# In an attention, routing and bilinear kernel, the split remainders and x transposes a unit later, w3 transposes in every second unit

## The chip, the cores and the metric

The kernel runs on one core of a Trainium2 chip. The metric is device microseconds (us) of one execution, here the median over several executions. The engines are named as in the profile: PE (TensorE matmul), DVE (VectorE), ACT (ScalarE), POOL (GpSimd) and SP (SyncE, which here only issues transfers).

## The reference

Four steps follow each other: windowed causal attention, a routed expert network (each of 2304 tokens goes to one of 8 experts), and a bilinear layer. Cut to what matters:

```python
# q, k, v: (4, 8, 576, 64) f32; window 128, a slope per head
attn = softmax(where(mask, q @ k.T * scale + bias, -1e9)) @ v     # -> x (2304, 512)
e_idx = argmax(x @ w_gate + modality_bias[modality_id], axis=1)   # 8 experts
x = gate[:, None] * (relu(x @ w1[e_idx]) @ w2[e_idx])             # 512 -> 1024 -> 512
h = ((x @ m_w1) * (x @ m_w2)) @ m_w3                              # float64 weights, 1024 x 1024
out = (h @ m_wout).astype(float32)                                # 512 columns
```

The kernel multiplies the last two weights with each other first (W = m_w3 @ m_wout), and it does so in the gaps of the attention. This product is called pw below, its pieces w3 and wo.

## The kernel before

**Units.** The attention runs in 40 units, numbered 0 to 39. Unit `i` is `units[i] = (b, c, hq)`: batch `b`, chunk `c` of 128 query rows (the fifth chunk of a batch, `c = NF`, has 64), and four of the eight heads. Two units make a chunk, an even one and then an odd one. The loop has 42 rounds, and round `i` writes the work of several units, in this order: `scores` and `softmax` of unit `i` (tile S in PSUM; DVE adds the bias and takes the row minimum into p, L458; ACT takes the exponential, L463); in odd rounds `attend` of the two units before (tile av); `p_transposes` of unit `i-1` (PT, copied by ACT to pT); then jobs from tables, and the transposes of later work. On PE the order is that of the program: each matmul is tied behind the one before (`after_pe`). On DVE, ACT and POOL a scheduler sets the order, from its own plan of the times, within the data's needs. In the block stage behind the loop the scheduler orders PE too.

**Splits.** All products of fp32 tiles are made of a rounded high part and a remainder (names end in h and l). In the first nine chunks (`pe_lo`) the remainder of q and k is made on PE: `split_k` copies the high part on ACT (kTh, qTh, L351) and puts `split_rest` on the list `rests`; `split_rests()` later issues one matmul with a negative identity into the same PSUM tile (ktp<-kTh,id_k and qtp<-qTh,id_q), and ACT copies the rest out (kTl, qTl, L319). In later chunks DVE subtracts instead (kTl L304, qTl L306).

**Transposes of x.** Behind `attend` ACT copies av to xT (L517; the 64-row tail to xTt, L525). `chunk_done` puts `gate_logits` on the list `todo`: four transposes (xtp), the gate product (lg), then on DVE x, lr, ls and the logit. Behind the last tile of a group (`GROUPS`) it puts `route` there too: some 15 small DVE operations that end in hot_b and hcum, two small matmuls that count tokens (rk<-hot_b and rk<-hcum), and scatters on POOL. One entry of `todo` is taken a round.

**w3 pieces.** A piece `j` of 16 is loaded (`load_w3`, SP, 512 KB, three buffers raw_w shared with the wo pieces), converted from float64 (`cvt_w3`, four DVE operations L753, L757, L760, L763 and one POOL addition L766), transposed on PE (`w3_transposes`, tile w3tp) and split by ACT and DVE (w3h, w3l). `w_step` then is three matmuls into pw (56 steps in all; `W_STEPS` says how many a round has, 35 of them in the loop, and 21 behind it cover the latency of routing). `LEAD` says how many rounds ahead of its first step a piece is loaded, converted and transposed, and `READY` gives these rounds for the last pieces by hand.

**Buffers in PSUM.** The tag A has two buffers, which ktp, qtp, qktp, lg, w3tp and rk take in turn; S has two and a unit uses both; av and xtp share the one buffer of V; pw has G.

**Behind the loop** stand the expert blocks (ph, py), and then the bilinear layer (p, po).

Of the kernel before, what the change touches and what calls it, by code (L numbers as in the profile page):

```python
# [27 lines left out]
WO_AT = [4, 5, 7, 8, 10, 11, 13, 15]  # L28
TP_AFTER = 20
M_PRE = 3  # L30
LEAD = [4, 3, 1]
LATE = 5
HB = 8
EARLY, M_PER, W_PER = 3, 3, 2

EDGE_L, EDGE_R = 96, 992
JS, BT = (3, 1)
W_STEPS = [0, 0, 0, 0, 0, 0, 0, 0, 0, 0, 0, 0, 0, 1, 1, 1, 1, 1, 2, 1, 1, 1, 2, 1, 1, 1, 2, 1, 1, 1, 2, 1, 1, 1, 2, 1, 1, 1, 2, 1, 1, 1]

IDLE_TO, IDLE_N = 12, 2  # L40

PW_FIRST = 3
GROUPS = [[0, 4], [4, 5], [9, 4], [13, 3], [16, 1], [17, 1]]

READY = [(28, 31, 34), (29, 32, 36), (30, 33, None), (31, 34, None), (32, 35, None), (33, None, None)]


def f32(ap):
# [4 lines left out]
def kernel(  # L53
# [728 lines left out]
    def split_wout(g):  # L782
        x = to_f32(w_p, st_w.pop(("o", g)), f"wo_{g}", x=wo_last if g == NG else None)
        if g < NG:
            nc.scalar.copy(woh[:, g, :], x)
            nc.gpsimd.tensor_tensor(
                out=wol[:, g, :], in0=x, in1=f32(woh[:, g, :]), op=ALU.subtract
            )

    def load_w3(i):  # L790
        fc, u = divmod(i, 2)
        st_w["3", i] = load_f64(
            w_p, m_w3[fc * P : (fc + 1) * P, u * HALF : (u + 1) * HALF], f"w3_{i}"
        )

    def cvt_w3(i):
        st_w["x", i] = to_f32(w_p, st_w.pop(("3", i)), f"w3_{i}")

    def w3_transposes(i, sp=split):
        x = st_w.pop(("x", i))  # L800
        h = w_p.tile([P, 4, P], F32R, tag="w3h", name=f"w3h_{i}", bufs=3)
        l = w_p.tile([P, 4, P], F32R, tag="w3l", name=f"w3l_{i}", bufs=3)
        tp = pst("A", [P, 4, P], f"w3tp_{i}")
        for j in range(4):
            pe(
                tp[:, j, :], lhsT=x[:, j * P : (j + 1) * P], rhs=ident, is_transpose=True,
                start=(j == 0 or sp is split), stop=(j == 3 or sp is split),
            )
        n = 3 if i % 2 else 4
        if i % 2:  # L810
            last["a"] = nc.scalar.copy(w3_last[:, i // 2, :], tp[:, 3, :])
        sp(h[:, :n, :], l[:, :n, :], tp[:, :n, :])
        st_w["T", i] = (h, l)

    def w_piece(k):

        fc, g = divmod(k, NG)
        return 2 * fc + g // 4, g % 4 == 0
# [96 lines left out]
    def chunk_done(b, c):  # L915
        if c == NF and b % 2 == 0:
            return
        i = tidx[b, c]
        g, j = tile_group[i]
        todo.append(lambda: gate_logits(i, g, j))  # L920
        if j == groups[g][1] - 1:
            todo.append(lambda: route(g, *groups[g]))
# [5 lines left out]
    def at(i, f, jobs=w_jobs):  # L928
        jobs.setdefault(max(i, 0), []).append(f)

    for g in range(NMC):
        if g >= WO_PRE:
            at(WO_AT[g] - 2, lambda g=g: load_wout(g))
        at(WO_AT[g], lambda g=g: split_wout(g))
    ks = 0
    for i, m in enumerate(W_STEPS):
        for _ in range(m):
            j, first = w_piece(ks)
            if first:
                if j >= W3_PRE:  # L940
                    at(i - LEAD[0], lambda j=j: load_w3(j))
                at(i - LEAD[1], lambda j=j: cvt_w3(j))
                at(i - LEAD[2], lambda j=j: w3_transposes(j), w_tps)
            at(i, lambda n=ks: w_step(n), w_steps)
            ks += 1
    n_w, k_in = NMC * NG, ks
    j_in, n_j = w_piece(k_in - 1)[0] + 1, 2 * NMC
    assert w_piece(k_in) == (j_in, True) and j_in + len(READY) == n_j
    for r, (u_load, u_cvt, u_tp) in enumerate(READY):
        at(u_load, lambda j=j_in + r: load_w3(j))  # L950
        if u_cvt is not None:
            at(u_cvt, lambda j=j_in + r: cvt_w3(j))
        if u_tp is not None:
            at(u_tp, lambda j=j_in + r: w3_transposes(j), w_tps)
    def idle(i):
        if i <= IDLE_TO:
            idle_work(IDLE_N)
# [6 lines left out]
            jobs.pop(i, None)  # L964

    for i in range(nu + 2):
        if 1 <= i < nu:
            scores(*units[i])
            softmax(*units[i])
        if i % NQ == 1 and i >= 3:  # L970

            for u in (units[i - 3], units[i - 2]):
                attend(*u)
            chunk_done(*units[i - 2][:2])
        if 1 <= i < nu + 1:
            p_transposes(*units[i - 1])
        with tc.issue_after(last["sm"].ins):
            run(w_jobs, i)
        run(w_steps, i, 1)

        ci = i // NQ + 1 if i > 1 else i
        if i and (i == 1 or i % NQ == 0) and ci < len(chunks):
            transposes(*chunks[ci])
            idle(i)
            run(w_steps, i, 1)
        if i % NQ == 1 and i // NQ + 2 < len(chunks):
            load_chunk(*chunks[i // NQ + 2])
        for f in extras.pop(i, []):
            f()
        if i % NQ:  # L990
            idle(i)
        if todo:
            todo.pop(0)()
        split_rests()
        run(w_tps, i)
        run(w_steps, i)
    strict[0] = False
    pe_mark = last["pe"]
# [403 lines left out]
```

## Time and profile before

| | |
|---|---|
| median of 3 executions | 792.93 us (790.63 to 793.63) |
| the profiled execution | 785.28 us, of it the span of the trace 783.5 us |
| PE busy | 742.3 us, 95% of the span |
| attention and routing | 0 to about 250 us; expert blocks 250 to 474; bilinear layer to the end |

A window of the trace gives each engine's busy time in a stretch, a row of waits says which engine waited for what, and a row of the timeline gives start, length and, in brackets, the idle time of the engine just before it with what ended it. Starts are counted from the start of the span.

### The profile page before, as it was taken

Reading aid. Unit: us, or ns where it says so; the run is one execution under the profiler, and the core shown is the slowest. Engines: PE = TensorE matmul, PEld = TensorE weight load, DVE = VectorE, ACT = ScalarE, POOL = GpSimd, SP = SyncE. Lnnn points to the kernel's source line nnn. Section 1 sums busy time; section 2 is a strip of 40 time slices with the busy share of each in tenths; the row PEclk is TensorE's granted clock in tenths of the full one; section 3 lists DMA queues with packets and bytes.
Section 4 is the critical chain, followed back from the end, with each engine's and each line's share of the span. In section 5 each row is a group of like instructions: output and inputs, shape, how many; then the busy total and the mean of one; then the engine's idle time right before and its main releaser. Section 6 shows DMA issues by size and latency. Waiting matters only on the chain. (4 is left out here: it accounts for less than half of the span.)

```text
span 783.5 us, 11943 instructions
## 1 busy us (share of the span) xinstructions
PE 742.3 (95%) x4424; PEld 618.2 (79%) x4424; DVE 388.8 (50%) x1015; ACT 325.7 (42%) x757; POOL 111.3 (14%) x140
## 2 busy tenths in 40 slices
PE   7898898996999999999999999999999999999996
PEld 4775786884877888888888885888888888888895
DVE  4687877787874575666666416550221122022030
ACT  6776767675645334333434224541222122122121
POOL 3235211213232220200100000001000000100101
PEclk9998999998999999999999999999999999999998
DMA  7866555455316765573844014002002001100000
GB/s 160 219 180 162 155 152 139 112 145 99 119 29 186 238 210 189 173 244 116 259 157 164 27 41 122 0 9 87 13 1 81 27 1 37 44 1 1 40 15 27
DMA packets 100503, 81.93 MB, mean 105 GB/s; under 512 B 69850, under 2 KB 83418, under 8 KB 100437
## 3 DMA queue, kind: packets, MB, share of 16 engines
q1 hardware_dynamic: 93925, 66.52, 30.0%
q0 software_dynamic: 3632, 9.66, 3.7%
q10 hardware_dynamic: 2880, 4.92, 1.7%
q8 instruction: 36, 0.59, 0.3%
q14 instruction: 30, 0.25, 0.1%
HBM read 66.36 MB, written 14.54 MB: 103 GB/s over the span
## 5 line engine op out<-in xcount | busy, mean ns | idle before, releaser
L1294 DVE TENSOR_TENSOR a<-a,p 128x512 f32<-128x512 f32 (+1 forms) x40 | 25.4, 634 | 188.8 <-PE p L293 188.8
L304 DVE TENSOR_TENSOR fwl<-fw,fwh 128x1024 fp32r<-128x1024 f32 x40 | 48.8, 1225 | 75.9 <-ACT fwh L302 66.0
L463 ACT ACTIVATE p<-p,mn 128x256 f32<-128x256 f32 (+2 forms) x144 | 67.9, 474 | 29.0 <-DVE mn L458 26.7
L302 ACT ACTIVATE fwh<-fw 128x1024 fp32r<-128x1024 f32 x40 | 42.2, 1061 | 89.1 <-PE ph L293 66.9
L293 PE MATMUL ph<-xbh,fwh 128*128 128x480 f32 x160 | 61.3, 384 | 0.0
L293 PE MATMUL ph<-xbh,fwl 128*128 128x480 f32 x160 | 61.0, 381 | 0.0
L293 PE MATMUL ph<-xbl,fwh 128*128 128x480 f32 x160 | 60.8, 380 | 0.0
L293 PE MATMUL py<-hl,fwh 128*128 128x480 f32 x160 | 60.4, 381 | 0.0
L302 ACT ACTIVATE abh<-a 128x512 fp32r<-128x512 f32 (+1 forms) x40 | 23.5, 588 | 87.2 <-DVE a L1294 87.2
L293 PE MATMUL p<-x2h,m0h 128*128 128x512 f32 (+1 forms) x160 | 59.0, 369 | 0.0
L293 PE MATMUL p<-x2l,m0h 128*128 128x512 f32 (+1 forms) x160 | 58.8, 368 | 0.0
L293 PE MATMUL p<-x2l,m1h 128*128 128x512 f32 (+1 forms) x160 | 58.8, 368 | 0.0
L293 PE MATMUL p<-x2h,m1l 128*128 128x512 f32 (+1 forms) x160 | 58.8, 368 | 0.0
L293 PE MATMUL p<-x2h,m0l 128*128 128x512 f32 (+1 forms) x160 | 58.8, 368 | 0.0
L293 PE MATMUL p<-x2h,m1h 128*128 128x512 f32 (+1 forms) x160 | 58.7, 368 | 0.0
L293 PE MATMUL py<-hh,fwl 128*128 128x480 f32 x160 | 57.9, 380 | 0.0
L293 PE MATMUL py<-hh,fwh 128*128 128x480 f32 x160 | 57.6, 379 | 0.0
L293 PE MATMUL po<-Wl,abh 128*128 128x512 f32 (+1 forms) x152 | 57.3, 378 | 0.0
L293 PE MATMUL po<-Wh,abh 128*128 128x512 f32 (+1 forms) x152 | 57.3, 378 | 0.0
L293 PE MATMUL po<-Wh,abl 128*128 128x512 f32 (+1 forms) x152 | 56.8, 378 | 0.0
L1316 POOL DMA_INDIRECT out_dram<-o,idg x17 | 16.4, 964 | 279.2 <-ACT o L1311 274.7
L458 DVE CUSTOM_DVE_ANT_0 p<-S,bias 128x256 f32<-128x256 f32 (+1 forms) x128 | 42.7, 384 | 13.8 <-PE S L293 13.2
(230 smaller groups left out, 1630.8 us busy)
## 6 DMA issues: line engine op xcount, KB each, us to landing
fw<-in_moe_w_dram SPq DMA_DIRECT2D x40, 512.0 KB, 4.9
raw_w<-in_moe_w_dram SPq DMA_DIRECT2D x16, 512.0 KB, 4.0
raw_m<-in_moe_w_dram SPq DMA_DIRECT2D x16, 512.0 KB, 3.7
ys_dram<-y ACTq DMA_DIRECT2D x20, 240.0 KB, 4.3
vr<-in_v_dram SPq DMA_DIRECT2D x16, 256.0 KB, 3.3
raw_wo<-in_moe_w_out_dram SPq DMA_DIRECT2D x8, 512.0 KB, 3.8
xs_dram<-x SPq DMA_DIRECT2D x16, 256.0 KB, 3.4
yt<-ys_dram SPq DMA_DIRECT2D x8, 512.0 KB, 4.5
```

Source lines behind the costliest of these rows:

```text
L293: last["pe"] = nc.tensor.matmul(*args, **kw)
L302: last["a"] = nc.scalar.activation(out=hi, in_=src, func=AF.Copy, scale=scale)
L304: last["v"] = nc.vector.tensor_tensor(out=lo, in0=src, in1=f32(hi), op=ALU.subtract)
L458: last["sm"] = nc.vector.tensor_tensor_reduce(out=p[:, j, t, :nk], in0=s[j][:, t, :nk], in1=bi, scale=1.0, scalar=BIG, op0=ALU.add, op1=AL ...
L463: nc.scalar.activation(out=p[:, j, t, :nk], in_=p[:, j, t, :nk], func=AF.Exp, scale=-1.0, bias=m1, accum_out=sm[:, col : col + 1],)
L1294: nc.vector.tensor_tensor(out=a[:, :nt], in0=a[:, :nt], in1=pp[1][:, :nt], op=ALU.mult)
L1316: sc = nc.gpsimd.indirect_dma_start(out=dst, out_offset=bass.IndirectOffsetOnAxis(ap=idx, axis=0), in_=o[:, ds_], in_offset=None,)
```

## The change

The work is the same but for two fillers (`idle`) that are left out in round 1. The round is written in another order: `split_rests()` is called in the odd rounds behind `p_transposes`, so one round later than the transposes it belongs to (in round 1 it stays in its round); `chunk_done` moves from the head of the odd round to its end, so `gate_logits` comes in the next even round and `route` in the odd round behind that; `w3_transposes` come in odd rounds alone, ahead of the next chunk's transposes. The tables `LEAD`, `W_STEPS` and `READY` are others: loads are issued two rounds ahead of the conversion and in the order of the pieces, steps begin with two in odd rounds and one in even ones, and of the last rounds some have none.

```diff
-LEAD = [4, 3, 1]
+LEAD = [5, 3, 1]
-W_STEPS = [0, 0, 0, 0, 0, 0, 0, 0, 0, 0, 0, 0, 0, 1, 1, 1, 1, 1, 2, 1, 1, 1, 2, 1, 1, 1, 2, 1, 1, 1, 2, 1, 1, 1, 2, 1, 1, 1, 2, 1, 1, 1]
+W_STEPS = [0, 0, 0, 0, 0, 0, 0, 0, 0, 0, 0, 0, 0, 2, 1, 2, 1, 2, 1, 2, 1, 2, 1, 2, 1, 2, 1, 2, 1, 2, 1, 2, 1, 1, 0, 1, 0, 0, 0, 1, 1, 1]
-READY = [(28, 31, 34), (29, 32, 36), (30, 33, None), (31, 34, None), (32, 35, None), (33, None, None)]
+READY = [(26, 29, 31), (28, 30, 33), (29, 31, 35), (30, 32, None), (31, 33, None), (32, 34, None), (33, None, None)]
...
-                at(i - LEAD[2], lambda j=j: w3_transposes(j), w_tps)
+                at((i - LEAD[2] - 1) | 1, lambda j=j: w3_transposes(j), w_tps)
...
     for i in range(nu + 2):
+        odd = i % NQ == 1
         if 1 <= i < nu:
             scores(*units[i])
             softmax(*units[i])
-        if i % NQ == 1 and i >= 3:
+        if odd and i >= 3:
             for u in (units[i - 3], units[i - 2]):
                 attend(*u)
-            chunk_done(*units[i - 2][:2])
         if 1 <= i < nu + 1:
             p_transposes(*units[i - 1])
         with tc.issue_after(last["sm"].ins):
             run(w_jobs, i)
+        if odd:
+            split_rests()
         run(w_steps, i, 1)
-
+        if todo:
+            todo.pop(0)()
+        run(w_tps, i)
         ci = i // NQ + 1 if i > 1 else i
-        if i and (i == 1 or i % NQ == 0) and ci < len(chunks):
+        if i and (i == 1 or not odd) and ci < len(chunks):
             transposes(*chunks[ci])
             idle(i)
-            run(w_steps, i, 1)
-        if i % NQ == 1 and i // NQ + 2 < len(chunks):
+            if i == 1:
+                split_rests()
+        elif odd:
+            idle(i)
+        if odd and i >= 3:
+            chunk_done(*units[i - 2][:2])
+            if i > nu:
+                run(w_steps, i)
+                while len(todo) > 1:
+                    todo.pop(0)()
+        if odd and i // NQ + 2 < len(chunks):
             load_chunk(*chunks[i // NQ + 2])
         for f in extras.pop(i, []):
             f()
-        if i % NQ:
-            idle(i)
-        if todo:
-            todo.pop(0)()
-        split_rests()
-        run(w_tps, i)
         run(w_steps, i)
```

In the order lists below a name has its tile and a running number; PT_1_0 is chunk 1 and the first half of its heads.

**First place: PE, units 2 and 3 (batch 0).** Before, behind the transposes of chunk 2 (ktp, qtp) in unit 2:

```order
L298 MATMUL PT_0_1_1_326<-ident,p_0_1_247 128x128 x2
L293 MATMUL ktp_2_0_332<-ident,kr_2_285 128x128 x4
L293 MATMUL qtp_2_0_338<-ident,qr_2_283 128x128 x4
L293 LDWEIGHTS ones_b
L293 MATMUL idle<-ones_b 128x512
L293 LDWEIGHTS ones_b
L293 MATMUL idle<-ones_b 128x512
L293 MATMUL ktp_2_0_332<-kTh_182,id_k 128x512
L293 MATMUL qtp_2_0_338<-qTh_2_343,id_q 128x512
L293 MATMUL S_1_1_1_376<-kTh_182,qTl_1_278 128x256
```

Now, in unit 3, with the scores of chunk 2 (S_2_0) as the next work behind:

```order
L298 MATMUL PT_1_0_0_407<-ident,p_1_0_308 128x128 x4
L298 MATMUL PT_1_0_1_413<-ident,p_1_0_308 128x128 x4
L293 MATMUL ktp_2_0_329<-kTh_182,id_k 128x512
L293 MATMUL qtp_2_0_335<-qTh_2_340,id_q 128x512
L293 LDWEIGHTS ones_b
L293 MATMUL idle<-ones_b 128x512
L293 LDWEIGHTS ones_b
L293 MATMUL idle<-ones_b 128x512
L293 MATMUL S_2_0_1_451<-kTh_182,qTl_2_341 128x256
```

The two remainder matmuls have moved from two fillers behind their transposes to a whole unit behind them; the distance from them to the scores that read qTl has gone from a unit to two fillers.

**Second place: PE and DVE, units 10 and 11 (batch 1), where the first group is routed.** PE before, in unit 11; the other half of rk, on hcum, stands behind the scores of unit 12:

```order
L609 LDWEIGHTS tri_b
L609 MATMUL rk_1024<-hot_b,tri_b 128x32
L293 MATMUL av_4_1067<-pT_4_1_964,vr_3_432 64x64 x2
L293 MATMUL av_4_1067<-pT_4_1_964,vr_4_615 64x64 x2
L293 MATMUL av_4_1067<-pT_4_1_964,vr_3_432 64x64 x2
L293 MATMUL av_4_1067<-pT_4_1_964,vr_4_615 64x64 x2
L298 MATMUL PT_0_0_0_1087<-ident,p_0_0_954 128x128 x2
```

PE now, in unit 11:

```order
L298 MATMUL PT_0_0_1_1053<-ident,p_0_0_933 128x128 x2
L293 MATMUL ktp_1_0_988<-kTh_836,id_k 128x512
L293 MATMUL qtp_1_0_994<-qTh_1_999,id_q 128x512
L609 LDWEIGHTS tri_b
L609 MATMUL rk_1091<-hot_b,tri_b 128x32
L612 LDWEIGHTS ones_b
L612 MATMUL rk_1091<-hcum,ones_b 128x32
L293 MATMUL w3tp_1108<-ident,x_w_0_962 128x128 x4
```

DVE before, ahead of the softmax of unit 10 (p_0_0):

```order
L549 TENSOR_TENSOR x_921<-xtp_922,r_3_898 128x512
L554 TENSOR_TENSOR lr_933<-lg_927,r_3_898 128x64
L557 TENSOR_REDUCE ls_934<-lr_933 128x8
L571 TENSOR_TENSOR logit_453<-ls_934,bmod 128x8
L587 TENSOR_REDUCE mx_1010<-logit_453 128x4
L588 TENSOR_TENSOR dd_1006<-logit_453,mx_1010 128x32
L458 ISA p_0_0_954,mn_0_0_955<-S_0_0_1_940,bias 128x128
```

DVE now, behind that softmax, among the conversions of a wo piece (w_wo) and of w3 piece 0 (w_w_0):

```order
L549 TENSOR_TENSOR x_970<-xtp_971,r_3_893 128x512
L757 SCALAR_TENSOR_TENSOR w_wo_950<-raw_wo_814,w_wo_950 128x512
L757 SCALAR_TENSOR_TENSOR w_w_0_960<-raw_w_0_816,w_w_0_960 128x512
L554 TENSOR_TENSOR lr_982<-lg_976,r_3_893 128x64
L760 TENSOR_SCALAR p_wo_951<-w_wo_950 128x512
L557 TENSOR_REDUCE ls_983<-lr_982 128x8
L763 SCALAR_TENSOR_TENSOR x_wo_952<-raw_wo_814,p_wo_951 128x512
L571 TENSOR_TENSOR logit_498<-ls_983,bmod 128x8
L760 TENSOR_SCALAR p_w_0_961<-w_w_0_960 128x512
L587 TENSOR_REDUCE mx_1077<-logit_498 128x4
L763 SCALAR_TENSOR_TENSOR x_w_0_962<-raw_w_0_816,p_w_0_961 128x512
L588 TENSOR_TENSOR dd_1073<-logit_498,mx_1077 128x32
```

The last tile's logits have moved behind the softmax of unit 10 while the counts on PE have moved ahead of the scores of unit 12. Both parts of rk now stand in a row.

**Third place: PE, units 33 and 34 (batch 3).** Before, in unit 34, the w3 piece 10 is transposed behind the transposes of chunk 3:

```order
L293 MATMUL ktp_3_0_2921<-ident,kr_3_2839 128x128 x4
L293 MATMUL qtp_3_0_2928<-ident,qr_3_2837 128x128 x4
L293 MATMUL pw_2584<-woh,w3h_2862 128x512
L293 MATMUL pw_2584<-wol,w3h_2862 128x512
L293 MATMUL pw_2584<-woh,w3l_2863 128x512
L293 MATMUL w3tp_2942<-ident,x_w_10_2683 128x128 x4
L293 MATMUL S_2_1_1_2950<-kTh_2424,qTl_2_2762 128x256
```

Now, in unit 33, with no ktp or qtp in the same unit:

```order
L298 MATMUL PT_1_0_1_2882<-ident,p_1_0_2789 128x128 x4
L293 MATMUL pw_2770<-woh,w3h_2558 128x512
L293 MATMUL pw_2770<-wol,w3h_2558 128x512
L293 MATMUL pw_2770<-woh,w3l_2559 128x512
L293 MATMUL w3tp_2903<-ident,x_w_10_2610 128x128 x4
L293 MATMUL S_2_0_1_2917<-kTh_2479,qTl_2_2834 128x256
```

The transposes of a piece have moved from one step behind ktp and qtp, whose A buffer they take, to a unit behind them. In the expert blocks and the bilinear layer the order of PE is unchanged.

## Rows read from the trace of the kernel before

**Rows 1.** The page: busy time, share of the span and instructions of each engine.

```profile
PE 742.3 (95%) x4424; PEld 618.2 (79%) x4424; DVE 388.8 (50%) x1015; ACT 325.7 (42%) x757; POOL 111.3 (14%) x140
```

**Rows 2.** Windows: start and end, length, busy time of PE, PEld, DVE, ACT, POOL.

```profile
9.50:56.60 47.10, 41.44 (x380) 32.98 (x380) 30.58 (x116) 36.97 (x109) 11.65 (x14) 0.96 0.75 186
56.60:74.60 18.00, 14.46 (x114) 10.37 (x113) 14.02 (x60) 12.53 (x41) 8.25 (x7) 0.81 0.70 191
74.60:175.60 101.00, 91.84 (x917) 77.96 (x915) 78.34 (x309) 71.44 (x223) 21.05 (x23) 1.00 0.51 134
175.60:202.50 26.90, 19.40 (x165) 16.34 (x164) 22.40 (x63) 15.59 (x46) 10.27 (x9) 0.87 0.56 128
202.50:250.00 47.50, 44.33 (x342) 35.96 (x341) 29.89 (x142) 23.69 (x63) 13.84 (x17) 1.00 0.31 92
250.00:783.50 533.50, 524.26 (x2485) 441.41 (x2483) 208.21 (x310) 160.17 (x260) 38.78 (x38) 1.00 0.27 87
```

**Rows 3.** Waits of PE from 0 to 250: us in total, times, longest.

```profile
PE w3tp L293 <- DVE kTl L304: 7.0, 2, 6.3
PE ktp L293 <- ACT kTh L351: 6.2, 6, 1.5
PE xtp L298 <- ACT xT L517: 5.4, 7, 1.6
PE w3tp L293 <- issue: 3.0, 1, 3.0
PE qtp L293 <- ACT qTh L351: 2.4, 3, 1.5
PE xtp L298 <- ACT xTt L525: 1.1, 1, 1.1
```

**Rows 4.** Timeline of PE: first scores of units 1, 10 and 13.

```profile
9.50 0.33 PE L293 MATMUL S<-kTh,qTl 64*128 64x128 f32 x2 [1.03 <-ACT qTl L319]
...
56.66 0.33 PE L293 MATMUL S<-kTh,qTl 64*128 64x128 f32 x2
...
74.65 0.39 PE L293 MATMUL S<-kTh,qTl 64*128 64x256 f32 x2
```

**Rows 5.** Timeline of DVE, units 10 to 12: softmax of unit 10, first and last hcum.

```profile
57.88 0.29 DVE L458 CUSTOM_DVE_ANT_0 p<-S,bias 128x128 f32<-128x128 f32 x1
...
62.51 1.23 DVE L605 TENSOR_TENSOR hcum<-hcum,hot_b 128x8 bf16<-128x8 bf16 x1
...
67.80 0.15 DVE L605 TENSOR_TENSOR hcum<-hcum,hot_b 128x8 bf16<-128x8 bf16 x1
```

**Rows 6.** Timeline of SP, unit 34: the issue of three w3 loads.

```profile
184.35 12.63 SPq L740 DMA_DIRECT2D raw_w<-in_moe_w_dram  x3
```

**Rows 7.** Timeline of DVE, unit 34.

```profile
190.38 0.76 DVE L753 TENSOR_SCALAR w_w<-raw_w 128x512 int32<-128x512 int32 x2 [3.24 <-DMA raw_w<-in_moe_w_dram]
191.06 1.29 DVE L757 SCALAR_TENSOR_TENSOR w_w<-raw_w,w_w 128x512 int32<-128x512 int32 x2
192.26 0.42 DVE L760 TENSOR_SCALAR p_w<-w_w 128x512 int32<-128x512 int32 x1
192.59 0.69 DVE L304 TENSOR_TENSOR kTl<-ktp,kTh 128x512 fp32r<-128x512 f32 x1
```

**Rows 8.** Timeline of PE, unit 34.

```profile
193.43 1.09 PE L293 MATMUL w3tp<-ident,x_w 128*128 128x128 f32 x4 [6.26 <-DVE kTl L304]
```

**Rows 9.** Groups on DVE from 0 to 250: busy us, mean ns, idle before.

```profile
L763 DVE SCALAR_TENSOR_TENSOR x_w<-raw_w,p_w 128x512 f32<-128x512 uint32 x16 | 11.2, 698 | 0.2
L549 DVE TENSOR_TENSOR x<-xtp,r 128x512 f32<-128x512 f32 x16 | 11.0, 686 | 4.0 <-PE xtp L298 3.6
L753 DVE TENSOR_SCALAR w_w<-raw_w 128x512 int32<-128x512 int32 x16 | 8.0, 510 | 5.0 <-DMA raw_w<-in_moe_w_dram 4.3 <-POOL x_w L766 0.8
```

**Rows 10.** Windows as in rows 2, within the stretches with PE's clock (third figure from the end) at half.

```profile
62.10:68.80 6.70, 6.70 (x63) 5.21 (x61) 6.70 (x23) 3.45 (x13) 4.19 (x3) 0.50 0.72 218
191.80:198.50 6.70, 5.07 (x40) 4.55 (x42) 6.42 (x16) 2.03 (x7) 2.71 (x2) 0.50 0.32 101
```

More of the change, by code (lines that the diff above doesn't have):

```diff
@@ L934 @@
         at(WO_AT[g], lambda g=g: split_wout(g))
+    n_j = 2 * NMC
+    j_rd = n_j - len(READY)
     ks = 0
@@ L938 @@
             j, first = w_piece(ks)
-            if first:
+            if first and j < j_rd:
                 if j >= W3_PRE:
@@ L946 @@
     n_w, k_in = NMC * NG, ks
-    j_in, n_j = w_piece(k_in - 1)[0] + 1, 2 * NMC
-    assert w_piece(k_in) == (j_in, True) and j_in + len(READY) == n_j
+    j_in = w_piece(k_in - 1)[0] + 1
+    assert w_piece(k_in) == (j_in, True) and j_rd <= j_in
     for r, (u_load, u_cvt, u_tp) in enumerate(READY):
-        at(u_load, lambda j=j_in + r: load_w3(j))
+        at(u_load, lambda j=j_rd + r: load_w3(j))
         if u_cvt is not None:
-            at(u_cvt, lambda j=j_in + r: cvt_w3(j))
+            at(u_cvt, lambda j=j_rd + r: cvt_w3(j))
         if u_tp is not None:
-            at(u_tp, lambda j=j_in + r: w3_transposes(j), w_tps)
+            at(u_tp, lambda j=j_rd + r: w3_transposes(j), w_tps)
     def idle(i):
```

## The prediction, made before the changed kernel ran

> **What bounds the kernel now.** I read the page's busy times first, then windows by stage, then the waits of the engine that is nearly full. PE is busy for 95% of the span [rows 1], but the rest is not spread evenly: behind 250 us PE idles 533.5 - 524.3 = 9.2 us in two thirds of the span, while the five windows from 9.5 to 250 leave it idle for 240.5 - 211.5 = 29 us [rows 2]. The change touches this first part alone, and the order of PE behind it stays. So the question is how much of 29 us goes.
>
> The waits say what these idle times are [rows 3]. Three kinds make up most: the remainders ktp and qtp wait for ACT's high parts (6.2 + 2.4 = 8.6 us); the transposes xtp wait for ACT's copy of av (5.4 + 1.1 = 6.5); w3tp waits for its PSUM buffer (7.0 + 3.0 = 10.0; the 3.0 that the profile calls issue is of the same kind, since kTl and qTl had just been read by DVE there). Together 25.1 us. In all three PE stands right behind a result that another engine has only just been given the input for. This is what the new order takes apart.
>
> But DVE is the second thing to see. From 175.6 to 202.5, units 33 to 35, DVE is busier than PE (22.4 against 19.4 us), and from 56.6 to 74.6, units 10 to 12, it is about as busy (14.0 against 14.5) [rows 2]. Where DVE has more to do than PE, taking PE's waits away only moves them.
>
> **The change, part by part.**
>
> *Remainders a unit later.* In units 2, 4, 8 and 14 the wait goes whole: a unit of scores, attend and PT lies between, and ACT has made kTh and qTh long before. Units 10 to 12 I count apart, since PE idles 18.0 - 14.5 = 3.5 us there [rows 2] for the same reason; what is left is 8.6 - 3.5 = 5.1 us gained. What is late next: the scores of the next even unit read qTl, which ACT can only write behind this matmul. With nothing between, scores waited 1.03 us for it [rows 4]; now two fillers stand between, but two copies of PT are ahead on ACT. I take 0.8 us in each of units 4, 6 and 10, where no w_step stands between: 2.4 us (bounds 0 and 3.1). Queued behind this wait are the softmax and everything of that unit.
>
> *x transposes a unit later.* xT is copied in the odd unit and read in the next even one, behind scores, PT and a step. The 6.5 us go. What could come instead: xtp takes the buffer that av needs in the unit after, so x must have been read by DVE within lg, ktp, qtp and the scores, some 3 us. DVE's x takes 0.69 us [rows 9], and it is hidden unless DVE is over 2 us late. Without that cover it costs up to 1 us in 16 places; I take nothing here, and count DVE's lateness below.
>
> *w3 transposes in odd units.* Then ktp and qtp are a unit old and their buffers free, and the 10.0 us go. The largest, 6.26 us in unit 34 [rows 8], has a cause further back: DVE idled 3.24 us for a load, and kTl stood in its queue behind two conversions [rows 7]; the load was late because SP stood 12.63 us over three issues, each waiting for a raw_w buffer [rows 6]. The new tables load the pieces in the order of their conversion and two rounds ahead, so a buffer is free a round before its load. In round 10 one load still waits for a conversion of the same round; behind it stand a chunk's loads that are needed two rounds later, so this costs nothing. Behind the 6.26 us PE ran at half its clock until 198.5 [rows 10]; half of the 5.07 us that it was busy would go, 2.5, if nothing idles as long again. I take half of that, 1.3.
>
> *Conversions.* None is added. Each is 0.51 + 0.69 + 0.42 + 0.70 = 2.3 us of DVE [rows 7, 9]. But seven stand in units 28 to 34 now, one in each, where the new steps are few. From 74.6 to 175.6 are 20 units (13 to 32) with 11 conversions: DVE 78.3, so (78.3 - 25.3)/20 = 2.65 us a unit without them, and PE 91.8/20 = 4.6 [rows 2]. Units 28 to 34 then hold 7 x 2.65 + 7 x 2.3 = 34.7 us for DVE and 7 x 4.6 = 32.2 for PE. DVE is never full for long: 83% in units 33 to 35 [rows 2], 96 to 100% in short stretches [rows 10]. At 100% the excess is 2.5 us, at 83% it is 34.7/0.83 - 32.2 = 9.6. I take 7 us given back, most of it ahead of rk in unit 31 and of qtp in unit 34 (A's buffer waits for lr). For units 22 to 25, a route of five tiles with two conversions, I take 1 more.
>
> *Units 10 to 12.* Before, DVE went from the softmax of unit 10 at 57.88 to the last hcum at 67.95, 10.1 us [rows 5]. Now x, lr, ls, logit, mx and dd lie in that stretch too, 0.69 + some 1.1 us, and two small ones: 12.2. The softmax can begin 0.5 us behind the scores, so the last hcum comes 12.7 us behind the start of unit 10, and only then rk, w3tp, fillers and the scores of unit 12, at 13.8; unit 12 itself shrinks to ACT's 3.6 (eight operations of 0.45). Together 17.4, where 74.65 - 56.66 = 18.0 is [rows 4]. So the 3.5 us of waits there turn into one in front of rk, and 0.6 us is gained (bounds: 6.9 if DVE keeps up, 3.5 of idle time and half the 6.7 us at half clock [rows 10]; 3 lost if POOL stands in its way).
>
> The row of 1.23 us for an hcum that elsewhere takes 0.15 [rows 5] shows what that means: POOL was adding a wo piece at the time. The Trainium skill (SBUF — State Buffer, section Who interferes with whom) says of this that DVE operations with two SBUF inputs and a GpSimd operation that reads SBUF exclude each other for a whole instruction. By that rule five POOL operations in these two units could add five times about 1.1 us to DVE's chain, and the kernel would gain 5 us less, 785; by the rows the stretch before holds such locks already, and the sum keeps them as they are.
>
> **Sum.** 5.1 - 2.4 + 6.5 + 10.0 + 1.3 - 7 - 1 + 0.6 = 13.1 us. The profiled execution took 785.28 us, and would take 772; the median of the runs is 792.93, 1.0% above it, and from that I take the same 13: **780 us**.
>
> **The rivals.** *DVE keeps up:* the list of DVE interleaves better than I fear, nothing is given back in units 10 to 12 and 28 to 34: 5.1 - 2.4 + 6.5 + 10.0 + 2.5 + 6.9 = 28.6, so 764 us. For it: from 74.6 to 175.6 DVE is busy 78% with PE at 91% [rows 2]. Against: both stretches in which DVE passes PE.
>
> *DVE takes it all back:* the waits go to rk, qtp and S instead, with 9.6 us in units 28 to 34, 3 lost in 10 to 12 and 3.1 at the scores: 5.1 - 3.1 + 6.5 + 10.0 - 9.6 - 3 - 3 (x late for av) = 3, so 790. For it: DVE at 100% in the half-clock stretch [rows 10].
>
> *Slower, by the counts on PE:* both halves of rk now stand on PE ahead of a w3tp and the next scores, and PE passes nothing. Its place is unit 11, and in the same way 23, 31 and the end of the loop. I price it 5.5 us in unit 11 (hcum at 12.7, PE there at about 7.2), already in the sum. If all four cost 5.5, and each puts PE at half clock with some 3 us lost as in [rows 10], that is three times 8.5 more, less the 8 counted: 17 us, hence 797. It decides from 13 us more on. Against: in the later routes the scheduler has put the second half of rk a unit behind the first.
>
> **How the numbers follow.** The forecast 0.50 (773 to 787 of its own), DVE keeps up 0.20, takes it back 0.18, slower 0.12. The range goes from 767, near the second case, to 791, beyond the third, and leaves out half of the second and most of the fourth. About 0.5%, 4 us, is what runs of this kernel tell from no change. Faster 0.71, same 0.18, slower 0.11.
>
> **What would show it.** Right: waits of ktp and qtp for kTh under 1 us in total outside unit 1, none of xtp for xT, none of w3tp for kTl; SP's L740 issues short; new waits of PE: S for qTl (about 2 us), rk for hcum or hot_b (5 in unit 11, 3 in unit 31), qtp for lr in unit 34; the first expert product (ph) 13 us earlier. The prediction is wrong if rk waits at all four routes, or if DVE idles in units 28 to 34 while PE waits for it, or if nothing waits for DVE there at all.

## The result: 1.1% slower, and the profile after

The changed kernel took 801.48 us (median of 5 executions, 798.47 to 801.58) where the kernel before took 792.09 us (median of 5, 787.9 to 793.63): a ratio of 1.0114, with an interval of 1.0078 to 1.0150. (A ratio compares all executions and can differ by up to 0.3% from the quotient of two medians.) The forecast was 780 us, with a range of 767 to 791. The profiled execution took 801.52 us with a span of 799.8, so it is a usual one. That of before (785.28 us) is 7 us under its median, so a difference between the two profiles can be that much too large.

The page of the changed kernel, with the row that answers to [rows 1], and three starts of units on PE (1, 10 and 13) that answer to [rows 4]:

```profile
PE 749.0 (94%) x4422; PEld 625.6 (78%) x4422; DVE 393.4 (49%) x1015; ACT 327.5 (41%) x757; POOL 112.3 (14%) x140
```

```profile
9.50 0.33 PE L293 MATMUL S<-kTh,qTl 64*128 64x128 f32 x2 [1.03 <-ACT qTl L319]
...
65.36 0.33 PE L293 MATMUL S<-kTh,qTl 64*128 64x128 f32 x2 [0.81 <-ACT qTl L319]
...
86.84 0.39 PE L293 MATMUL S<-kTh,qTl 64*128 64x256 f32 x2
```

From unit 1 to unit 10 it is 55.9 us now and was 47.2; from unit 10 to 13 it is 21.5 and was 18.0. So 12 us are lost before unit 13, in the part where waits were to go. The first expert product starts at 268.5 and started at 252.0; the other 4.3 us are lost between. Behind it both kernels take 531.4 to 531.5 us.

The waits of PE from 0 to 250, against [rows 3] (us in total, times, longest):

```profile
PE S L293 <- ACT qTl L319: 8.8, 5, 4.4
PE qtp L293 <- DVE lr L554: 7.2, 6, 2.2
PE rk L609 <- ACT kTl L319: 5.9, 1, 5.9
PE rk L609 <- DVE hot_b L600: 4.2, 3, 2.5
PE PT L298 <- ACT p L463: 4.0, 2, 3.5
PE w3tp L293 <- POOL x_w L766: 2.6, 1, 2.6
PE w3tp L293 <- ACT kTl L319: 2.5, 2, 1.5
...
PE ktp L293 <- ACT kTh L351: 0.3, 1, 0.3
```

The waits that the change was made against are gone but for 0.3 us (ktp, qtp for ACT's high parts, xtp for xT, w3tp for DVE's kTl), 25 us of them, and these rows stand in their place. The second difference is PE's clock. Windows inside the stretches at half clock, against [rows 10] (third figure from the end is the granted clock):

```profile
25.00:31.00 6.00, 4.15 (x24) 3.92 (x25) 2.08 (x11) 3.74 (x10) 0.00 (x0) 0.50 0.74 202
42.00:48.00 6.00, 6.00 (x32) 5.10 (x32) 2.57 (x11) 3.67 (x12) 0.78 (x1) 0.50 0.26 85
59.00:62.00 3.00, 3.00 (x24) 2.83 (x25) 2.06 (x9) 1.46 (x6) 0.71 (x1) 0.50 0.97 253
80.00:86.00 6.00, 5.63 (x30) 4.43 (x30) 3.62 (x14) 2.89 (x9) 4.77 (x4) 0.50 0.26 88
196.00:198.50 2.50, 2.50 (x17) 1.97 (x14) 1.80 (x10) 0.85 (x4) 0.00 (x0) 0.50 0.31 123
209.30:218.70 9.40, 9.16 (x56) 8.61 (x58) 6.62 (x21) 5.83 (x18) 1.17 (x1) 0.50 0.07 28
```

Each of the six stretches begins inside a wait of PE or within 1.5 us of its end: S until 26.9 and until 40.3, qtp until 57.8, rk until 79.9 and until 193.9, PT until 208.6. Not every wait has one behind it: w3tp's 2.6 us, until 159.3, has none. With the one at 11 us these are 41 us at 1.2 GHz ahead of the expert blocks, where before had 17.

What the 4.4 us in unit 4 wait for is seen in the timeline of ACT and PE from 21.3 us on (start, length; the remainder matmuls of chunk 2 are the first two rows):

```profile
21.31 0.48 PE L293 MATMUL ktp<-kTh,id_k 128*128 128x512 f32 x1
21.63 0.40 PE L293 MATMUL qtp<-qTh,id_q 128*128 128x512 f32 x1
...
22.30 0.51 ACT L463 ACTIVATE p<-p,mn 128x256 f32<-128x256 f32 x1 [1.67 <-DVE mn L458]
...
24.26 0.51 ACT L463 ACTIVATE p<-p,mn 128x256 f32<-128x256 f32 x1
...
24.77 1.05 ACT L484 COPY pT<-PT 128x512 f32<-128x512 f32 x2
...
25.71 0.60 ACT L319 ACTIVATE kTl<-ktp 128x512 fp32r<-128x512 f32 x1
...
26.20 0.60 ACT L319 ACTIVATE qTl<-qtp 128x512 fp32r<-128x512 f32 x1
26.85 0.58 PE L293 MATMUL S<-kTh,qTl 64*128 64x256 f32 x2 [4.38 <-ACT qTl L319]
```

The matmuls are done at 22.0 and ACT is idle then, but it goes by its list: four exponentials of unit 3, xT and two copies of PT stand ahead of kTl and qTl, and the exponentials wait for DVE's softmax. DVE's softmax in turn stands behind four small operations on the modality ids, and these wait for their load (POOL's mid_f starts at 20.49):

```profile
20.71 0.46 DVE L258 TENSOR_SCALAR inv<-mid_f 128x18 f32<-128x18 f32 x1 [2.58 <-POOL mid_f L254]
...
21.78 0.42 DVE L458 CUSTOM_DVE_ANT_0 p<-S,bias 128x256 f32<-128x256 f32 x1
```

So a part of the 4.4 us belongs to this load. The run below with remainders early in unit 11 alone has the same order of instructions on PE, DVE, ACT and POOL up to unit 11. Its unit 3 began 1.9 us later, mid_f was there by then, and S in unit 4 waited 2.6 us:

```profile
27.02 0.39 PE L293 MATMUL S<-kTh,qTl 64*128 64x256 f32 x2 [2.59 <-ACT qTl L319]
```

In the kernel before the same copies of chunk 2 stood ahead of that softmax:

```profile
20.90 0.60 ACT L319 ACTIVATE kTl<-ktp 128x512 fp32r<-128x512 f32 x1
21.38 0.61 ACT L319 ACTIVATE qTl<-qtp 128x512 fp32r<-128x512 f32 x1
22.57 0.51 ACT L463 ACTIVATE p<-p,mn 128x256 f32<-128x256 f32 x1 [0.58 <-DVE mn L458]
```

And unit 11, against [rows 5]: rk takes the A buffer that ktp held, and so waits for kTl; kTl stands on ACT behind the softmax of unit 11, and that on DVE behind the route. DVE and POOL first, then DVE's softmax and last hcum, then ACT and PE:

```profile
71.54 1.65 DVE L763 SCALAR_TENSOR_TENSOR x_w<-raw_w,p_w 128x512 f32<-128x512 uint32 x1
...
73.26 1.27 POOL L766 TENSOR_TENSOR x_w<-x_w,w_w 128x512 f32<-128x512 f32 x1 [0.63 <-DVE x_w L763]
...
73.32 1.25 DVE L593 TENSOR_SCALAR cand<-dd 128x32 f32<-128x32 f32 x1
...
74.49 1.26 POOL L786 TENSOR_TENSOR wol<-x_wo,woh 128x512 fp32r<-128x512 f32 x1
74.60 1.20 DVE L596 TENSOR_TENSOR cand<-cand,iota_em 128x32 f32<-128x32 f32 x1
...
77.55 0.28 DVE L458 CUSTOM_DVE_ANT_0 p<-S,bias 128x128 f32<-128x128 f32 x1
...
79.01 0.16 DVE L605 TENSOR_TENSOR hcum<-hcum,hot_b 128x8 bf16<-128x8 bf16 x1
...
79.25 0.60 ACT L319 ACTIVATE kTl<-ktp 128x512 fp32r<-128x512 f32 x1
...
79.91 0.19 PE L609 MATMUL rk<-hot_b,tri_b 128*128 128x32 bf16 x1 [5.88 <-ACT kTl L319]
```

The loads did what they were to do: where SP stood 12.63 us over three issues [rows 6], the longest issue of a w3 load is 0.677 us now (shortest, median and longest in ns, first and last start):

```profile
L740 SPq DMA_DIRECT2D raw_w<-in_moe_w_dram x16: 334/344/677, 53.1 to 201.8; - x16
```

### The profile page after: what moved, and what is told of

It reads as the page before. It is cut to its first block, busy times and chain, and to the rows that moved or that the text cites. A ratio compares the mean times of both kernels' runs of the same rounds, so it can differ in the third digit from the quotient of the medians.

```text
span 799.8 us, 11947 instructions
## 1 busy us (share of the span) xinstructions
PE 749.0 (94%) x4422; PEld 625.6 (78%) x4422; DVE 393.4 (49%) x1015; ACT 327.5 (41%) x757; POOL 112.3 (14%) x140
## 5 line engine op out<-in xcount | busy, mean ns | idle before, releaser
L302 ACT ACTIVATE fwh<-fw 128x1024 fp32r<-128x1024 f32 x40 | 42.3, 1062 | 89.0 <-PE ph L293 66.8
```

What stands on the lines that cost most here:

```text
L302: last["a"] = nc.scalar.activation(out=hi, in_=src, func=AF.Copy, scale=scale)
```

## The experiments

Ratios are to the kernel before, run beside each on the same chip (its medians there lie between 787.66 and 789.40 us). The changed kernel has 1.0114.

### The parts of the change

**Remainders back in their own unit** (all else as changed):

```diff
-        if odd:
-            split_rests()
         run(w_steps, i, 1)
...
             idle(i)
-            if i == 1:
-                split_rests()
+            split_rests()
```

> The changed kernel, with the remainders of q and k back in the unit of their transposes (behind two fillers). Theory A (the loss is made by the late remainders: kTl and qTl come to stand behind a whole softmax on ACT, scores and rk wait for them 8.8 + 5.9 us, and PE's clock halves behind each such wait): these waits go, some 8 us of half clock too, and the 8.6 us of waits for kTh and qTh come back; about 787 us, S waits for qTl under 3 us, and rk no longer waits for kTl. Rival B (the loss is made by the late logits and routes: qtp waits for lr, rk for DVE's chain): no change, 798 or more. Rival C (the w3 tables load DVE too much): no change, 798 or more.

Measured: 787.76 us, 0.9990 (0.9962 to 1.0019). As theory A had it: S's waits for qTl fall to 1.5 us and none of rk for kTl is left. But ktp and qtp wait only 2.6 us for their high parts, not 8.6, and rk waits 6.5 us for hot_b instead. By this run the late remainders are what makes the change slower, and the rest of it gains nothing that the interval tells.

**Logits behind the transposes**, on top of that:

```diff
-        if todo:
+        if odd and todo:
             todo.pop(0)()
         run(w_tps, i)
...
             split_rests()
-        elif odd:
+        if not odd and todo:
+            todo.pop(0)()
+        if odd:
             idle(i)
```

> As the run with the remainders back, and the logits of the even rounds written behind the next chunk's transposes and remainders, not ahead of them, so that lg no longer takes the buffer that qtp needs (two fillers more in unit 1). Theory A: the 7.2 us that qtp waits for lr are a smaller term; they go, and the time is 3 to 6 us below the run with the remainders back, about 782. Rival B: this is the main term, 10 us or more below the run with the remainders back. Rival C: both stay near 798.

Measured: 808.67 us, 1.0261 (1.0211 to 1.0312), 21 us slower instead of 5 faster. The row of waits tells why:

```profile
PE lg L293 <- DVE kTl L304: 16.1, 7, 4.1
```

Tag A has two buffers, and ktp, qtp and lg want three in a row. Whichever comes third waits for what reads the first: qtp for lr (some 1 us each time), or lg for DVE's kTl (2.3 us). The order of the change is the cheaper of two.

**The w3 part alone**, on the kernel before: its three tables, the loads in the order of the pieces, and

```diff
-                at(i - LEAD[2], lambda j=j: w3_transposes(j), w_tps)
+                at((i - LEAD[2] - 1) | 1, lambda j=j: w3_transposes(j), w_tps)
```

> The kernel before, with the w3 part alone: new tables, loads in the order of the pieces, w3 transposes in odd rounds. Theory A: w3tp no longer waits for kTl (10 us in the kernel before) and the half clock of unit 34 goes, with some of it given back to DVE: 783 to 788 us. Rival B: the same. Rival C (new tables overload DVE in units 28 to 34): 796 or more, with PE waiting there for rk, PT or w3tp.

Measured: 787.89 us, 0.9976 (0.9945 to 1.0008). The time is theory A's, but the kernel before took 787.66 us on that chip, and the interval includes no difference at all. The 10 us of w3tp are gone, but another wait has grown, ktp for kTh in unit 14, from 1.5 to 3.2 us, and PE has 31 us at half clock before the expert blocks where the kernel before has 17. So much of what was taken from the waits seems to have gone into the clock; one profile of each does not show how much.

**Logits back**, in the odd round behind attend, and the route ahead of the transposes of the even round (remainders late and w3 tables as changed, the w3 transposes at the end of their odd round):

```diff
                 attend(*u)
+            chunk_done(*units[i - 2][:2])
...
-        if todo:
+        if not odd and todo:
             todo.pop(0)()
-        run(w_tps, i)
...
+        if odd and todo:
+            todo.pop(0)()
+        run(w_tps, i)
         run(w_steps, i)
```

> The changed kernel, with the logits back in the odd round behind attend, and the route in the even round ahead of the transposes; remainders late and w3 tables new, as in the changed kernel. Theory A: scores still wait for qTl (4 us in unit 4, 1 to 2 in units 6 and 10) and the clock still halves behind that; 794 to 800 us. Rival B (late logits are the loss): waits of qtp for lr and of rk go and xtp's 6.5 us come back; about 788. Rival C: 798 or more, with nothing but the waits of the first half moved.

Measured: 798.42 us, 1.0120 (1.0074 to 1.0165). The time is theory A's, but the mechanism wasn't what I had expected: S waits only 1.6 us, and it is lg that waits for kTl (4.2) and rk for hot_b and hcum (12.7). From the start of unit 1 to that of unit 9 it is 41.3 us here, against 49.1 in the changed kernel and 42.3 before. So this run has another loss, and doesn't clear the late logits: where xtp and lg stand between the late remainders and the next scores, units 1 to 8 lose nothing.

### Where on ACT, and what the clock costs

**Remainders right behind the scores** of the unit after their transposes, ahead of its softmax:

```diff
             scores(*units[i])
+            if odd:
+                split_rests()
             softmax(*units[i])
...
-        if odd:
-            split_rests()
         run(w_steps, i, 1)
```

> The changed kernel, with the remainders still in the unit behind their transposes, but right behind that unit's scores and ahead of its softmax, attend and PT. Theory A (it isn't the distance on PE that costs, but the place of the kTl and qTl copies on ACT, behind a softmax): kTl stands ahead of the exponentials on ACT now, S no longer waits more than 1 us for qTl in units 4 and 6, and the half clock behind it goes; the wait of rk in unit 11 for kTl goes too, but turns mostly into one for hcum or hot_b, which DVE has at nearly the same time. Some 1.007 of the kernel before, 3 to 5 us below the changed kernel. Rival D (any rest held over a unit costs, since it keeps both A buffers): no change, 1.011. Rival E (the price is PE's clock alone): as theory A, within what a run tells.

Measured: 788.61 us, 0.9993 (0.9969 to 1.0016): the whole loss is gone, more than expected, with the remainders on PE still a unit behind their transposes. ACT in unit 3:

```profile
20.76 0.60 ACT L319 ACTIVATE kTl<-ktp 128x512 fp32r<-128x512 f32 x1
...
23.53 0.51 ACT L463 ACTIVATE p<-p,mn 128x256 f32<-128x256 f32 x1 [2.17 <-DVE mn L458]
...
24.53 0.57 ACT L319 ACTIVATE qTl<-qtp 128x512 fp32r<-128x512 f32 x1
...
25.15 0.39 PE L293 MATMUL S<-kTh,qTl 64*128 64x256 f32 x2 [1.74 <-ACT qTl L319]
```

kTl stands ahead of the softmax and qTl behind its second exponential, not behind everything; S waits 1.7 us, not 4.4. With the row of ACT in the changed kernel that shows that the place on ACT is what costs: there PE was done with the remainders at 22.0 and S began at 26.9. The 1.7 us that are left, where under 1 was expected, go back to mid_f again, for which DVE idled 3.55 us until 21.9 here; in the run with units 3 to 9 early, below, mid_f was in time, and S in unit 4 waits less than half a us. rk in unit 11 waits 0.8 us, for hot_b.

**Fillers** where PE waited longest (the waits stay):

```diff
         elif odd:
             idle(i)
+            idle_work({3: 18, 5: 6}.get(i, 0))
...
+        if i == 11:
+            idle_work(24)
         if todo:
```

> The changed kernel, with fillers on PE where it waited longest in the first half: 18 more behind the two of unit 3, 6 more behind those of unit 5, 24 ahead of rk in unit 11 (about as long at full clock as the waits of 4.4, 1.7 and 5.9 us). The waits themselves stay, as ACT and DVE are what they were. If the half clock behind the waits is a good part of the loss (the changed kernel has 41 us of it from 0 to 250, the one before 17), the stretches at 24.6, 41.7 and 79.2 us shrink or go, and the time falls by 4 to 8 us, to 1.002 to 1.006 of the kernel before. If the waits alone are the loss: no change, or 1 to 2 us slower where a filler stands in the way.

Measured: 794.12 us, 1.0062 (1.0038 to 1.0085). Unit 3 still takes 8.0 us (8.4 in the changed kernel), unit 11 still 11.9 (11.4), but the clock stays up behind them. Units 4 (28.7 to 34.0) and 6, and a stretch at half clock in units 10 and 11 that the changed kernel doesn't have:

```profile
28.70:34.00 5.30, 4.82 (x45) 3.96 (x44) 4.23 (x16) 3.71 (x12) 0.00 (x0) 1.00 0.32 95
40.50:44.60 4.10, 4.10 (x40) 3.53 (x40) 2.81 (x12) 3.19 (x10) 1.74 (x2) 1.00 0.43 133
64.90:75.10 10.20, 9.26 (x65) 6.60 (x65) 10.02 (x34) 6.77 (x23) 4.21 (x4) 0.50 0.74 202
```

Unit 4 takes 5.3 us at full clock where it took 6.9. So filling three waits is worth 0.5%, 4 us, somewhat under half of the loss (the two intervals just overlap). That is the half clock behind them only in the main: 24 us of half clock are left, and PT's wait of 3.5 us in unit 34, with 10.2 us of half clock behind it, is not in this profile either, though no filler stands there.

**Remainders early, logits back:** the two edits together.

> The run with the logits back, with the remainders right behind the scores of the unit after their transposes. Theory A: lg no longer waits for kTl (4.2 us there); the waits of rk for hot_b and hcum (12.7 us there) are DVE's and stay; about 1.006 of the kernel before. Rival D: no change, 1.012.

Measured: 794.41 us, 1.0074 (1.0046 to 1.0103): lg's wait is gone, rk's 12.7 us are the same. What is left are these, 8.7 us of xtp for xT and xTt, and 41 us of half clock. Late remainders cost 0.5% here, less than the two intervals can tell, where they cost 1.2% in the changed kernel.

### Unit 11, and the conversions

**The route behind** the w3 transposes and fillers, on top of the remainders back:

```diff
-        if todo:
+        if todo and not odd:
             todo.pop(0)()
         run(w_tps, i)
...
         elif odd:
             idle(i)
+        if todo and odd:
+            todo.pop(0)()
```

> The run with the remainders back, and the route at the end of the odd round, behind the w3 transposes and fillers, not ahead of them. If what that run lost again lies in rk (6.5 us of waits for hot_b), these waits go, and the kernel gains 3 to 6 us over it: 0.993 to 0.996 of the kernel before, the first version faster than it. If DVE is full there, the wait moves on to the next scores, and nothing is gained: 0.999.

Measured: 784.77 us, 0.9959 (0.9937 to 0.9981), at the edge of what was expected. rk's 6.5 us are all but gone, and 0.3% of the time with them, 2.5 us; the rest came back as waits elsewhere (pw for wraw grew from 2.6 to 4.2 us, qtp for pr from 1.0 to 2.2).

**Both**, the route behind and the remainders right behind the scores:

> The run with the route behind, with the remainders right behind the scores of the next unit in place of their own unit. If kTl and qTl stand ahead of the softmax on ACT, the place on PE costs nothing (theory A): 0.995 to 0.997 of the kernel before, as the run with the route behind; a few tenths of a per cent less if the waits for kTh and qTh that are left there (1.8 us) go. If holding both A buffers over a unit costs (rival D): 1.000 or more.

Measured: 785.56 us, 0.9960 (0.9942 to 0.9977), as expected: a unit's distance on PE costs nothing if ACT's copies stand ahead of the softmax, and gains nothing.

**Conversions a round earlier**, on top of the route behind, two numbers: `LEAD = [6, 4, 1]` in place of `[5, 3, 1]`. This moves the nine pieces 0 to 8; the last seven go by `READY` and stay where they were, here and in the runs below.

> The run with the route behind, with w3 pieces loaded and converted one round earlier, transposes in the same rounds. If w3tp's 5.1 us of waits for POOL's x_w are conversions that come too late, they go, and the kernel gains 2 to 5 us more: 0.990 to 0.994 of the kernel before. If the conversions are late because DVE is full, they are late all the same, or push the softmax: 0.996 to 1.000.

Measured: 777.89 us, 0.9881 (0.9855 to 0.9908): 10 us faster than the kernel before, the best of all, and more than expected. w3tp's waits for x_w are gone (from 5.1), and so are 3 us of qtp's waits for lr, since a conversion no longer stands on DVE just where lr does; PE has 17 us at half clock. The largest of what is left is pw for wraw, 5.2 us; qtp for lr has 2.1.

**The same with the remainders early:**

> The run with the conversions a round earlier, with the remainders right behind the scores of the next unit in place of their own unit. With kTl and qTl ahead of the softmax on ACT the place of the remainders on PE is worth 0.1% or less either way (theory A): 0.986 to 0.990 of the kernel before. Rival D (held A buffers cost): 0.993 or more.

Measured: 780.62 us, 0.9904 (0.9875 to 0.9934), just above what was expected; from the run before it no clear difference.

**The changed kernel with `LEAD = [6, 4, 1]`** and nothing else:

> The changed kernel, with w3 pieces loaded and converted one round earlier and nothing else. Theory A: it gains what the conversions are worth by themselves, some 5 us behind unit 16, and keeps the late remainders' loss before unit 13 (S for qTl 8.8 us, rk for kTl 5.9): 1.003 to 1.007 of the kernel before. If the conversions were the cause of the loss (rival C): 0.997 or less.

Measured: 786.04 us, 0.9962 (0.9936 to 0.9988). A miss: 1.5% gained, not 0.6, and my theory that the late remainders alone are the cause fell short: with the remainders as late as in the changed kernel, it is no longer slower. rk in unit 11 waits 2.7 us for hot_b, not 5.9 for kTl. S still waits, but the clock doesn't fall behind it in this execution (24 to 31 us, with S's wait of 3.3 us inside):

```profile
27.33 0.38 PE L293 MATMUL S<-kTh,qTl 64*128 64x256 f32 x2 [3.33 <-ACT qTl L319]
```

```profile
24.00:31.00 7.00, 3.67 (x37) 3.35 (x36) 3.03 (x13) 5.41 (x16) 0.00 (x0) 1.00 0.78 209
```

Four more runs separate the places. **Remainders early and the conversions earlier:**

> The changed kernel, with the remainders right behind the scores and all w3 pieces converted a round earlier. If the two cures act on different waits, their gains add up: 1.0114 less 1.2% less 1.5%, so 0.984. If both act on one wait (rk in unit 11, where kTl stands on ACT behind a softmax that stands on DVE behind the route and piece 0), the gains overlap: 0.990 to 0.995.

Measured: 780.63 us, 0.9909 (0.9879 to 0.9938). The gains of 1.2 and 1.5% overlap by 0.7%: with the conversions earlier, late remainders cost 0.5% (0.9962 against 0.9909) and not 1.2.

**Piece 0 alone a round earlier** (`- (j == 0)` in the rounds of its load and its conversion):

> The changed kernel, with piece 0 alone loaded and converted a round earlier, in unit 9 and not 10. If unit 11 is where the conversions meet the late remainders, rk's wait of 5.9 us falls below 3 us as it did when all pieces came earlier, and the half clock of 79.2 us goes: 1.002 to 1.006 of the kernel before. If the later conversions made the gain: 1.010 or more.

Measured: 792.37 us, 1.0056 (1.0029 to 1.0084). From unit 10 to 13 it is 18.2 us, not 21.5, and rk waits 2.2 + 2.0 us for hcum. So piece 0 is worth 0.6%, 3.3 us of it there by these profiles. Behind unit 13 the two profiles differ by some 5 us more: PT waits 0.3 us for ACT and not 4.0, and 3.4 us from 209 on are at half clock and not 10.2. Whether piece 0 does that is not shown. The other eight pieces make the rest of the 1.5%. Where the remainders are early or back, the nine pieces together gain 0.6 to 0.8%.

**Remainders early in unit 11 alone** (`if i == 11: split_rests()` behind the scores):

> The changed kernel, with the remainders right behind the scores in unit 11 alone. If unit 11 holds most of the loss: 1.002 to 1.005 of the kernel before, rk waiting less than 2 us. If units 4 to 10 hold it: 1.008 or more.

Measured: 794.69 us, 1.0094 (1.0059 to 1.0128), hardly anything: rk still waits 4.1 us for kTl. On PE the remainders are early, but the scheduler put kTl on ACT behind two exponentials of unit 11 (73.79, 74.19; kTl at 74.58). So the edit didn't take the wait away, and doesn't tell what unit 11 is worth; it shows once more that the place on PE isn't the one that counts.

**Remainders early in units 3 to 9 alone** (`if odd and 3 <= i <= 9`):

> The changed kernel, with the remainders right behind the scores in units 3, 5 and 9 alone, so that the scores of units 4, 6 and 10 find qTl ready sooner, while rk in unit 11 still waits for kTl behind a softmax. If units 4 to 10 hold half of the loss: 1.004 to 1.007 of the kernel before. If unit 11 holds most: 1.008 or more.

Measured: 788.66 us, 1.0002 (0.9979 to 1.0026): nearly all of the gain that the remainders early have. Units 1, 10 and 13:

```profile
10.97 0.47 PE L293 MATMUL S<-kTh,qTl 64*128 64x128 f32 x2 [0.83 <-ACT qTl L319]
...
57.61 0.33 PE L293 MATMUL S<-kTh,qTl 64*128 64x128 f32 x2
...
77.23 0.58 PE L293 MATMUL S<-kTh,qTl 64*128 64x256 f32 x2
```

From unit 1 to 10 it is 46.6 us (55.9 in the changed kernel, 47.2 before), and from 10 to 13 still 19.6; rk in unit 11 waits 4.1 us, for hot_b. So the waits of S in units 4, 6 and 10, with the clock behind them, hold 1.1%, and unit 11 only some tenths (0.9993 with the remainders early in all odd units).

## Why the prediction was wrong, step by step

Forecast and result lie 22 us apart. Of these the remainders are some 12: the sum has 5.1 - 2.4 = 2.7 us gained for them, and putting them back shows 1.2%, 9.8 us, lost. The other 10 are the rest of the sum: it has 10.4 us gained, and the run with the remainders back shows about 1.

**Remainders a unit later: the step that failed.** The waits of ktp and qtp went as forecast (8.6 us became 0.3). "What is late next" named the right place, the scores of units 4, 6 and 10, but priced it by PE's distance and two copies of PT: 0.8 us each, bounds 0 to 3.1 in all. They were 4.4, 1.7 and 0.8, and ACT's own list decided: kTl and qTl stood behind a whole softmax. I had compared the orders of PE and DVE and never that of ACT at this place, though it is ACT that finishes the remainder. The bound from "nothing in between" wasn't an upper one, because ACT was held by DVE, and DVE in unit 3 by a load; some 1.8 of the 4.4 us are this load's (4.4 against 2.6). With the clock behind the waits this term was not -2.4 but some -9 us (1.1%, by the run with units 3 to 9 early). Without it the change is no loss; that it is one by itself can't be said, since earlier conversions take the loss away too, and late remainders cost units 1 to 8 nothing where the logits come early.

**Half clock: sign wrong.** I counted 1.3 us gained. The new waits brought 41 us of half clock for 17, and the fillers put three of these stretches at some 4 us. In the w3 part alone, 14 us more at half clock stand against what its waits gave.

**x transposes.** xtp waits for nothing any more, 6.5 us as forecast, but qtp for lr grew to 7.2 us in six places; I had seen it in unit 34 only. With two A buffers a wait for one of them goes on under another name, and no gain of this part can be told: the remainders back (w3 part and late logits) have 0.9990, the w3 part alone 0.9976.

**w3 transposes.** The 10.0 us for kTl went, and 5.5 came back at w3tp (x_w 2.6, kTl 2.5, qTl 0.4). The loads were right. "None of w3tp for kTl" was wrong, then. The conversions a round earlier remove the waits for x_w; that the new tables put them too near their transposes and into unit 10 was not in the sum.

**Units 10 to 12: place and size of the wait right, result wrong.** "5.5 in unit 11" for rk was measured as 5.88, partly by luck, since it was kTl that came last. But the length was to be 17.4 us and is 21.5: kTl was as late as hcum, which I hadn't followed, DVE lost 3 us to POOL, and 6.8 us ran at half clock. The run with piece 0 earlier has 3.3 us of it back.

**Units 22 to 34.** The size came as forecast, 8.2 us for the 8 that I had given back, the places in part: rk for hot_b in unit 31 (2.5) as named, qtp for lr in units 24 to 30 (0.8, 1.6 and 0.7) and not in unit 34, and w3tp for x_w in unit 25 (2.6), with DVE busy 25.95 of the 26.9 us from 175.6 on. The largest one there, 3.5 us of PT for ACT in unit 34, follows a late copy of av (below).

**The rivals.** "Slower, by the counts on PE" had the sign and the clock's part, with 797 us, but named the wrong place: unit 11 and three other routes, where units 4 to 10 hold most. "DVE takes it all back" is near what the change would be with the remainders put right: 790 us is 0.996 of the kernel before, and these runs have 0.9990 and 0.9993.

**What stays open.** Why the gains of early remainders and earlier conversions overlap by 0.7%. In the profile of the changed kernel with earlier conversions the clock stayed at 2.4 GHz from 24 to 48 us, though S waited 3.3 and 1.7 us. But no order differs there: up to unit 9, PE, DVE, ACT and POOL have the same order of instructions in the changed kernel, with piece 0 earlier, with unit 11 early and with the conversions earlier. From the start of unit 1 to that of unit 9 these four profiles take 49.1, 49.2, 46.1 and 44.9 us. With the remainders early or back it is 41.0 to 42.0 (44.5 where the logits stand behind the transposes), and 42.3 in the kernel before. So late remainders cost 3 to 8 us in these units, and how much differs between executions of the same orders. What the earlier conversions gain in these units can't be told from one profile.

## What to carry to other kernels

A step moved on one engine is finished by another that has an order of its own: read that engine's list at the new place, and ask what stands ahead of the finishing copy and what that in turn waits for. Two or three tiles in one ring of buffers pass a wait on from one to the other, so count it until it ends, not where it stood; and price a wait on PE with the clock behind it. Here two numbers, which convert nine pieces a round earlier, were worth more than the reordering, and with remainders in their own unit and the route behind the w3 transposes this made the kernel 1.2% faster.

## What the runs showed of the hardware that I had not expected

**The clock falls behind one wait and not behind another of the same length.** In the four profiles that have the same orders up to unit 9, S waited 1.7 us in unit 6 each time. Behind it came 6.8, 6.8 and 3.4 us at 1.2 GHz, and none in the run with earlier conversions. In unit 4 it waited 4.4, 4.5, 2.6 and 3.3 us, and behind it came 6.8, 6.8, 3.4 and none. With 18 fillers in the wait the clock stayed up. So one profile doesn't price the clock behind a wait.

**POOL's lock hit three DVE operations in unit 11,** the 1.65, 1.25 and 1.20 us above, against 0.69, 0.17 and 0.18 for such operations elsewhere in the two traces: 3 us, three of the five times that I had priced at 1.1. The row L593 is an operation with one tensor input. The Trainium skill (SBUF — State Buffer, section Who interferes with whom) names that case too: `tensor_scalar` can enter a mode that takes the shared ports. The trace agrees: 1.25 us beside POOL's addition of 1.27.

**PE's results reached ACT late while POOL issued the scatters of a route.** In unit 33 of the changed kernel av ended at 202.00, and ACT, idle from 202.5 on, copied it only at 206.45; four scatters of POOL, from 200.3 to 205.35, and an addition, from 205.38 to 206.65, fill that time. PE, POOL and ACT:

```profile
200.91 1.09 PE L293 MATMUL av<-pT,vr 128*64 128x128 f32 x16
```

```profile
203.12 0.96 POOL L627 DMA_INDIRECT ys_dram<-tg,pos_i  x1 [0.30 <-issue]
204.39 0.96 POOL L627 DMA_INDIRECT ys_dram<-tg,pos_i  x1 [0.31 <-issue]
```

```profile
206.45 0.59 ACT L517 COPY xT<-av 128x512 f32<-128x512 f32 x1 [3.93 <-PE S L293]
```

PT's wait of 3.5 us in unit 34 and the half clock from 209 on follow it. The kernel before has a smaller one: av ends at 177.79, ACT is done with an exponential at 179.1, and xT starts at 179.93, 0.80 us later. The last scatter ended at 179.03 there, and xtp in unit 33 waited 1.05 us. In the w3 part alone (ACT and DVE at 226.8) and the route behind (DVE at 228.3) PE's results came 1.3 to 1.4 us behind their end beside scatters of a route too. That the scatters cause them was not tried.
